# Gated mix of multi-query attention and a state-space convolution on one core: filler matmuls by a shorter history, a burst of dummy matmuls before the scores, two sines as two operations, and gate selectors with a later due time

## The chip, the cores and the metric

The kernel runs on one core of a Trainium2 chip. The metric is the device time of one execution in microseconds; the figure for the kernel before is the median of five executions.

## The reference

From one input x (2048 tokens, 448 channels) two results are computed and mixed by a gate per token.

```
q = (x @ wq) in 16 heads of 28;  k = x @ wk;  v = x @ wv      # one k and one v for all heads
a = softmax(q k^T / sqrt(28)) v, heads joined, @ wo
K[d, l] = Re( sum_n C[d,n] * exp(dt*A[d,n] * l) * dt*B[d,n] )  # 448 channels, 256 complex modes
b = causal convolution of x with K along the tokens + x * Dskip
g = sigmoid(sum(x * gate_w))
out = g * a + (1 - g) * b
```

## The kernel before, in words

Every operation is handed to a planner (class `Prog`) with its engine, an estimated duration, the keys that it reads and writes and a priority `pr` (the lower comes first). `schedule` plays the program through with these estimates and fixes one order for each engine; `emit` writes that order out with the semaphore waits that the keys demand. On the chip each engine then works through its list in order. If an instruction has to wait, everything behind it on that engine waits too.

**Attention.** The scores of 16 heads times 4 query blocks times 16 key tiles make 1024 tiles of 128 by 512. `qk` (L1069) multiplies two or three tiles into one of two PSUM areas (`psS`). One ScalarE instruction takes the exponential of the two or three tiles (L1079), 410 instructions in all. `pv` (L1087) multiplies four of them with v into `psB`, which gathers 16 key tiles of a head group; DVE then copies it out (L1032). `qproj` prepares q for a head group: four matmuls (L729), a reduction of absolute values on DVE into the buffer `Wk` (L734), one more matmul that gives a bound for the softmax (L736), and a copy to `qT` (L738).

**Convolution.** For each of 28 chunks of channels DVE builds tables of powers by doubling (`tables`, L811 to L831), TensorE multiplies them to the kernel K (`kgen`, L846), the result goes through DRAM, and TensorE applies it (`conv`, L914; `jpass`, L889). The planner works the chunks in between the scores. Ahead of this, `seeds_sin` and `seeds` compute sine, cosine and exponentials of dt*A.

**Start.** x is transposed (L541), k is projected (L654), ScalarE copies results out of PSUM (L549, L659). In `seeds_sin` DVE reduces the angle (L595 to L600) and takes its absolute value (L601); ScalarE takes the sine of the angle (L604) and the cosine as a sine of pi/2 less the absolute value (L605). Both sines are one operation for the planner, which starts when L601 is done. A change from Sine to Exp costs a table load on ScalarE.

**Filler.** While `psB` is open (from the first to the last `pv` of a head group), `schedule` puts dummy matmuls (`filler`, L975: four matmuls of zeros by 256 columns) into the planned idle time of TensorE. It does so where the columns worked in the last `FILL_WIN` ns are below `FILL_RATE` columns per ns (1.3 before 75 us of planned time), and where the planned gap is at least the cost of a filler (107 ns, and 112 ns for a change of tile shape) plus `FILL_GAP`.

**Gate.** `prep_gate` computes v and the gate (`mv`, L677), and 28 small matmuls (`mo`, L699 and L704) select and permute the gate values into PSUM bank 5; three DVE operations copy them out (L709, L711, L716), and two DMAs move one of the copies. `conv` uses the same bank later, and its results are scaled by `omq`.

Of the kernel before, what the change touches and what calls it, by code (L numbers as in the profile page):

```python
# [7 lines left out]
AF = mybir.ActivationFunctionType  # L8
# [3 lines left out]
P = 128  # L12
# [6 lines left out]
DT = 112  # L19
# [29 lines left out]
def dram(t, off, dims):  # L49
    return bass.AP(tensor=t.tensor, offset=t.offset + off, ap=[list(d) for d in dims])  # L50
# [7 lines left out]
class Prog:  # L58
# [3 lines left out]
    SWITCH = 112.0  # L62
    LAT = {"pe": 175.0, "act": 105.0, "dve": 105.0}
    LOOK, LOOK_END = {"dve": 200.0}, 26e3
    FILL_NS, FILL_MAC, FILL_WIN, FILL_RATE, FILL_GAP = 107.0, 256.0, 3413.0, 0.47 * 2.4, 130.0
    FILL_WARM = 75e3

    def __init__(self, nc, es):
# [261 lines left out]
def el(n, rate=0.96, fix=69):  # L330
    return fix + n / rate


class Kernel:
# [10 lines left out]
    def build(self):  # L345
        nc = self.nc
        with self.es:
            self.pg = Prog(nc, self.es)
            self.pg.filler = self.filler
            self.alloc()  # L350
            self.consts()
            self.loads()
            self.prep_x()
            self.seeds_sin()
            self.prep_attn()
            self.qproj(0, 0)
            self.seeds()
            self.prep_gate()
            self.main()
            self.pg.schedule()  # L360
            with nc.Block() as block:
                self.pg.emit(block)
# [218 lines left out]
    def seeds_sin(self):  # L581
        pg = self.pg
        self.fT, self.fO, self.fM = self.T.cast(F32), self.O.cast(F32), self.mbf.cast(F32)
        W2 = 2 * D
        t = lambda j: self.tf(j)[0].v(0, P, self.tf(j)[1], [[1, W2]])
        tt = lambda j: self.tf(j)[0].v(0, P, self.tf(j)[1], [[D, 2], [1, D]])
        K = self.tk
        dtb = self.dt32.v(0, P, 0, [[0, 2], [1, D]])
        pg.op("act", lambda e: e.activation(self.fT.v(0, P, 0, [[1, D]]), self.dt32.v(0, P, 0, [[1, D]]), AF.Exp), 600,
              rd=["dt"], wr=[K(0)], pr=-1)  # L590
        pg.op("dve", lambda e: e.tensor_copy(self.dt32.v(0, P, 0, [[1, D]]), self.fT.v(0, P, 0, [[1, 2], [224, 2], [2, DT]])), 540,
              rd=[K(0)], wr=["dt"], pr=-0.5)
        p1, k1, _ = self.trans(1, 6)
        ns = el(W2)
        TT = lambda e, o, a, b, op: e.tensor_tensor(o, a, b, op)  # L595
        pg.op("dve", lambda e: TT(e, tt(1), p1, dtb, ALU.mult), ns, rd=[k1, "dt"], wr=[K(1)], pr=-0.5)
        pg.op("dve", lambda e: e.tensor_scalar(t(2), t(1), 1.0 / TWO_PI, MAGIC, ALU.mult, ALU.add), ns / 2, rd=[K(1)], wr=[K(2)], pr=-0.5)
        pg.op("dve", lambda e: e.tensor_scalar(t(2), t(2), -MAGIC, -TWO_PI, ALU.add, ALU.mult), ns / 2, rd=[K(2)], wr=[K(2)], pr=-0.5)
        pg.op("dve", lambda e: TT(e, t(1), t(1), t(2), ALU.add), ns, rd=[K(1), K(2)], wr=[K(1)], pr=-0.5)
        pg.op("dve", lambda e: e.tensor_scalar(t(1), t(1), -math.pi, math.pi, ALU.max, ALU.min), ns / 2, rd=[K(1)], wr=[K(1)], pr=-0.5)  # L600
        pg.op("dve", lambda e: e.scalar_tensor_tensor(t(2), t(1), -1.0, t(1), ALU.mult, ALU.max), ns, rd=[K(1)], wr=[K(2)], pr=-0.5)  # L601

        def sins(e):
            e.activation(t(3), t(1), AF.Sin)  # L604
            return e.activation(t(4), t(2), AF.Sin, bias=self.small.v(0, P, 3, [[1, 1]]), scale=-1.0)  # L605
        pg.op("act", sins, 4500, rd=[K(1), K(2), "hpi"], wr=[K(3), K(4)], pr=-1)

    def seeds(self):
        pg = self.pg
# [60 lines left out]
    def prep_gate(self):  # L670
        pg = self.pg
        xT = self.xT

        def mv(e):
            for kt in range(16):
                for T in range(NT):
                    r = e.matmul(self.psB.v(0, P, 32 * kt, [[1, 29]]), xT.v(0, DT, T * S + 128 * kt, [[1, 128]]),  # L677
                                 self.Wv.v(0, DT, T * 32, [[1, 29]]), start=(T == 0), stop=(T == 3), tile_position=(0, 0))
            return r
        pg.op("pe", mv, 1900, rd=["Wv"] + [k for c in range(4) for k in self.xk(512 * c)], wr=[("b", 6)], pr=-0.2)  # L680
        pg.op("dve", lambda e: e.tensor_copy(self.vaug.v(0, P, 0, [[32, 16], [1, 28]]),
                                             self.psB.v(0, P, 0, [[32, 16], [1, 28]])), el(448),
              rd=[("b", 6)], wr=["va", ("b", 6)], pr=-0.2)
        gv, ov = self.gtok.v(0, P, 0, [[1, 16]]), self.gtok.v(0, P, 16, [[1, 16]])
        pg.op("act", lambda e: e.activation(ov, self.psB.v(0, P, 28, [[32, 16]]), AF.Tanh, scale=0.5), 150,
              rd=[("b", 6)], wr=["gt"], pr=-0.6)
        pg.op("dve", lambda e: e.tensor_scalar(gv, ov, 0.5, 0.5, ALU.mult, ALU.add), 80, rd=["gt"], wr=["gt"], pr=1.2)
        hi, lo = self.gb.v(0, P, 0, [[1, 16]]), self.gb.v(0, P, 16, [[1, 16]])
        pg.op("dve", lambda e: e.tensor_copy(hi, gv), 80, rd=["gt"], wr=["gb"], pr=1.2)
        pg.op("dve", lambda e: e.tensor_tensor(lo, gv, hi, ALU.subtract), 80, rd=["gt", "gb"], wr=["gb2"], pr=1.2)  # L690
        t, o = self.bank(5)

        def mo(e):
            for k in range(3):
                for rr in range(2):
                    sel = self.J.v(0, P, 64 * rr, [[1, 64]]) if k == 0 else self.ident.v(0, P, 64 * rr - (k - 1), [[1, 64]])
                    for z in range(2):
                        for par in range(2):
                            r = e.matmul(t.v(64 * par, 64, o + 32 * k + 16 * rr, [[1, 16]]), sel,  # L699
                                         self.gb.v(0, P, 16 * z, [[1, 16]]), start=(z == 0), stop=(z == 1),  # L700
                                         tile_position=(0, 64 * par), skip_group_check=True)
            for z in range(2):
                for par in range(2):
                    r = e.matmul(t.v(64 * par, 64, o + 96, [[1, 16]]), self.J.v(0, P, 64 * par, [[1, 64]]),  # L704
                                 self.gb.v(0, P, 16 * z, [[1, 16]]), start=(z == 0), stop=(z == 1),
                                 tile_position=(0, 64 * par), skip_group_check=True)
            return r
        pg.op("pe", mo, 800, rd=["id", "J", "gb", "gb2"], wr=[("b", 5)], pr=1.7, mode="c64")
        pg.op("dve", lambda e: e.tensor_copy(self.gm.v(0, P, 0, [[1, 2], [2, 16]]), t.v(0, P, o, [[16, 2], [1, 16]])), 100,  # L709
              rd=[("b", 5)], wr=["gm"], pr=1.7)  # L710
        pg.op("dve", lambda e: e.tensor_copy(self.gn.v(0, P, 0, [[1, 16]]), t.v(0, P, o + 96, [[1, 16]])), 90,  # L711
              rd=[("b", 5)], wr=["gn"], pr=1.7)
        pg.dma([(dram(self.G, 0, [[1, P], [P, 16]]), self.gn.v(0, P, 0, [[1, 16]]))], (2048, 4), "gw", rd=["gn"], wr=["G"], pr=5, slow=True)
        pg.dma([(self.gn.v(32 * h, 32, 16, [[1, 16]]), dram(self.G, 1536, [[16, 32], [1, 16]])) for h in range(4)],
               (128, 64), "gd", rd=["G"], wr=["gd"], pr=5)
        pg.op("dve", lambda e: e.tensor_scalar(self.omq.v(0, P, 63, [[-32, 2], [-1, 2], [-2, 16]]), t.v(0, P, o + 32, [[32, 2], [16, 2], [1, 16]]),  # L716
                                               -1.0, 1.0, ALU.mult, ALU.add), 130, rd=[("b", 5)], wr=["omq"], pr=1.7)
# [482 lines left out]
```

## Time and profile before

| | |
|---|---|
| median of 5 executions | 524.04 us (521.77 to 524.5) |
| the profiled execution | 524.5 us, of which its span is 522.6 us |
| ACT (ScalarE) busy | 483.4 us, 92% |
| DVE (VectorE) busy | 471.8 us, 90% |
| PE (TensorE) busy | 465.3 us, 89% |
| granted TensorE clock, mean | 0.963 |
| filler matmuls (L975) | 1124 instructions |
| first exponential of the scores | at 27.76 us |

Times are from the start of the span. "Busy" of an engine counts its own instructions, not waits. The granted clock is the share of TensorE's full clock that the throttle let through. "Idle before" is the time for which an engine stood still ahead of an instruction, with what ended it.

### The profile page before, as it was taken

The numbers are of one execution on the slowest core, as the hardware profiler recorded it, in microseconds if no ns is written. First come the engines' busy times: TensorE is split into PE (matmuls) and PEld (weight loads), VectorE is DVE, ScalarE is ACT, GpSimd is POOL, SyncE is SP. The second block draws the span as 40 slices with busy tenths as digits, with TensorE's granted clock in tenths as the row PEclk, the third lists the DMA queues.
The fourth block names the chain that finished last, engine by engine and source line by source line (L and its number), as shares of the span: only waits on it lengthen the run. The fifth ranks groups of instructions, "written<-read, shape, count | busy, mean of one in ns | idle before, by whom it ended". The sixth has DMA issues, their size and how long they took to land.

```text
span 522.6 us, 20724 instructions
## 1 busy us (share of the span) xinstructions
PE 465.3 (89%) x9304; PEld 232.8 (45%) x9304; DVE 471.8 (90%) x1140; ACT 483.4 (92%) x428; POOL 7.5 (1%) x15
## 2 busy tenths in 40 slices
PE   4799888898999989989999899999989899999985
PEld 3442344354534445444444445444444444544434
DVE  4899999999989999999999999999999999997113
ACT  2587999999989999999999999999999999999991
POOL 5000000000000000000000000000000000000000
PEclk9965989999969989999999999999999999999999
DMA  9849700665456436645655765646576746835651
GB/s 196 175 109 125 108 9 11 220 196 175 138 167 179 108 120 193 168 153 140 163 170 150 199 179 165 180 77 186 167 208 171 199 145 178 241 126 189 221 115 37
DMA packets 119279, 80.43 MB, mean 154 GB/s; under 512 B 81825, under 2 KB 87142, under 8 KB 119190
## 3 DMA queue, kind: packets, MB, share of 16 engines
q1 hardware_dynamic: 118166, 78.62, 56.6%
q8 instruction: 73, 1.20, 1.0%
q10 hardware_dynamic: 1024, 0.48, 0.4%
q14 instruction: 16, 0.13, 0.1%
HBM read 73.26 MB, written 5.70 MB: 151 GB/s over the span
## 4 chain that ended last, share of the span: by engine, by line
DVE 53%; ACT 30%; PE 13%; DMA 1%; issue 1%; SPq 0%; DVEq 0%
ACT expT L1079 30%; DVE tab L821 10%; DVE tmp L811 8%; DVE tab L815 8%; DVE tab L829 4%; DVE tab L831 4%; PE psS L1069 3%; DVE cst L923 2%; PE psB L1087 2%; DVE msq L769 2%; PE psX L846 1%; DMA tab<-in_A_x_dram 1%; DVE acc L1032 1%; DVE Wk L734 1%; DVE qT L738 1%; DVE kstg L864 1%
## 5 line engine op out<-in xcount | busy, mean ns | idle before, releaser
L1079 ACT ACTIVATE expT<-psS 128x1536 bf16<-128x1536 f32 (+1 forms) x410 | 468.3, 1258 | 13.1 <-PE psS L1069 6.9
L1069 PE MATMUL psS<-qT,kT 29*128 29x512 bf16 x1024 | 164.4, 397 | 33.7 <-ACT expT L1079 27.9
L1087 PE MATMUL psB<-expT,vaug 128*32 128x512 bf16 x1024 | 104.5, 399 | 0.4 <-ACT expT L1079 0.4
L821 DVE TENSOR_TENSOR tab<-tab,tmp 128x64 bf16<-128x64 bf16 (+1 forms) x280 | 91.1, 365 | 0.8
L1069 PEld LDWEIGHTS psS<-qT,kT 29*128 29x128 bf16 x1024 | 39.4, 91 | 110.9 <-ACT expT L1079 87.4
L914 PE MATMUL psS<-T,U 128*64 128x64 bf16 (+7 forms) x3584 | 85.6, 195 | 0.3 <-issue 0.2
L914 PEld LDWEIGHTS psS<-T,U 128*64 128x64 bf16 (+7 forms) x3584 | 67.4, 107 | 35.1 <-issue 33.9
L811 DVE TENSOR_TENSOR tmp<-tab,mbf 128x128 bf16<-128x128 bf16 (+4 forms) x140 | 80.1, 572 | 0.8
L815 DVE TENSOR_TENSOR tab<-tab,mbf 128x128 bf16<-128x128 bf16 (+4 forms) x140 | 78.9, 569 | 0.0
L846 PE MATMUL psX<-tab 128*32 128x96 bf16 x1792 | 54.9, 267 | 2.4 <-DVE O L894 1.2
L1087 PEld LDWEIGHTS psB<-expT,vaug 128*32 128x32 bf16 x1024 | 26.3, 93 | 61.0 <-issue 59.7
L975 PE MATMUL psB<-kT,zw 128*32 128x256 bf16 x1124 | 50.4, 284 | 0.0
L846 PEld LDWEIGHTS psX<-tab 128*32 128x32 bf16 x1792 | 40.7, 115 | 16.3 <-issue 7.1
L829 DVE TENSOR_TENSOR tab<-tab,mbf 128x2048 bf16<-128x2048 bf16 x28 | 34.3, 1226 | 0.2
L831 DVE TENSOR_TENSOR tab<-tab,mbf 128x2048 bf16<-128x2048 bf16 x28 | 34.2, 1221 | 0.0
L975 PEld LDWEIGHTS psB<-kT,zw 128*32 128x32 bf16 x1124 | 26.9, 98 | 14.6 <-issue 11.3
L923 DVE TENSOR_TENSOR cst<-psS,omq 128x512 bf16<-128x512 f32 x28 | 19.2, 686 | 6.6 <-PE psS L914 6.6
L769 DVE TENSOR_TENSOR msq<-mst 128x448 f32<-128x448 f32 (+2 forms) x45 | 23.9, 531 | 0.0
L729 PE MATMUL psX<-xT,Wq 112*128 112x512 bf16 x64 | 21.3, 409 | 1.1 <-DVE O L618 0.7
L779 DVE CAST mbf<-mst 128x448 bf16<-128x448 f32 (+2 forms) x50 | 17.4, 348 | 0.0
L772 DVE TENSOR_TENSOR mst<-msq 128x224 f32<-128x224 f32 (+2 forms) x50 | 17.2, 345 | 0.0
L775 DVE SCALAR_TENSOR_TENSOR mst<-mst 128x224 f32<-128x224 f32 (+2 forms) x45 | 15.6, 346 | 0.0
(124 smaller groups left out, 270.2 us busy)
## 6 DMA issues: line engine op xcount, KB each, us to landing
T<-KP_scratch SPq DMA_DIRECT2D x224, 256.0 KB, 4.0
rdenB<-R_scratch SPq DMA_DIRECT2D x60, 64.0 KB
tab<-in_A_x_dram SPq DMA_DIRECT2D x8, 224.0 KB, 6.8
XD_scratch<-xT SPq DMA_DIRECT2D x8, 224.0 KB
U<-XD_scratch SPq DMA_DIRECT2D x7, 256.0 KB, 5.4
O<-Z_scratch SPq DMA_DIRECT2D x1, 1792.0 KB, 17.2
KP_scratch<-kstg SPq DMA_DIRECT2D x56, 32.0 KB
U<-XD_scratch SPq DMA_DIRECT2D x7, 192.0 KB, 5.4
```

Of the source, the lines that this page charges most:

```text
L769: pg.op("dve", lambda e, k=k: e.tensor_tensor(msq.v(0, P, 0, [[1, 2 * BW]]) if k > 1 else msq.v(0, P, 0, [[BW, 2], [1, BW]]), src_both(k - ...
L811: pg.op("dve", lambda e, a=src, ra=ra, w=w, so=so: e.tensor_tensor(tmp.v(0, P, so, [[4 * w, 32], [1, 4 * w]]), a, mbf.v(0, P, ra + 4, [[8, ...
L815: pg.op("dve", lambda e, d=dst, a=src, ra=ra, w=w: e.tensor_tensor(d, a, mbf.v(0, P, ra, [[8, 16], [0, 2 * w], [1, 4]]), ALU.mult), el(n, ...
L821: pg.op("dve", lambda e, d=d, t=t2, op=op: e.tensor_tensor(d, d, t, op), el(n // 2, 1.92), rd=[("tmp", lv % 2), ("tab", s, lv + 1)], wr=[( ...
L829: pg.op("dve", lambda e: e.tensor_tensor(ua, src, mbf.v(0, P, ra, [[8, 8], [0, 64], [1, 4]]), ALU.mult), el(2048, 1.92), rd=rk + mk, wr=[( ...
L831: pg.op("dve", lambda e: e.tensor_tensor(ub, src, mbf.v(0, P, ra + BC * 64, [[4, 16], [0, 32], [1, 4]]), ALU.mult), el(2048, 1.92), rd=rk ...
L846: r = e.matmul(self.psX.v(32 * g, 32, 96 * jj, [[1, 96]]), tab.v(0, P, o + 768, [[4, 32]]), tab.v(0, P, o, [[256, 3], [4, 32]]), start=(jj ...
L914: r = e.matmul(ps.v(64 * par, 64 - m, po + 64 * pr, [[1, 64]]), self.U.v(0, P, uo + (32 * par + e0 + pr) * UC + m, [[1, 64 - m]]), self.T. ...
L975: e.matmul(self.psB.v(32 * h, 32, 0, [[1, 256]]), self.zw.v(0, P, 0, [[1, 32]]), self.kT.v(0, P, 0, [[1, 256]]), start=False, stop=False, ...
L1069: r = e.matmul(self.psS.v(0, P, 1536 * s + 512 * k, [[1, 512]]), kT.v(32 * h, DH + 1, 128 * kt, [[1, 128]]), qT.v(32 * h, DH + 1, 512 * qs ...
L1079: pg.op("act", lambda e: e.activation(expT.v(0, P, 512 * (i0 % 10), [[1, n]]), self.psS.v(0, P, 1536 * s, [[1, n]]), AF.Exp, scale=SQ), 61 ...
L1087: r = e.matmul(self.psB.v(32 * h, 32, 0, [[1, 512]]), vaug.v(0, P, 32 * kt, [[1, 32]]), expT.v(0, P, 512 * ((4 * st + h) % 10), [[1, 512]] ...
```

## The change

The constants of the filler rule change. A new function `warm`, called after the first `qproj`, hands the planner five operations of two 512-column matmuls each, whose result in `psB` nobody reads; they read `Wk`, x and the last quarter of k. The two sines become two operations: the first needs the angle alone, the second the absolute value and the first sine. The gate selectors `mo` get a slack of 4000 ns, by which the planner takes their inputs to be ready later than they are.

```diff
-    FILL_NS, FILL_MAC, FILL_WIN, FILL_RATE, FILL_GAP = 107.0, 256.0, 3413.0, 0.47 * 2.4, 130.0
+    FILL_NS, FILL_MAC, FILL_WIN, FILL_RATE, FILL_GAP = 107.0, 256.0, 1700.0, 0.55 * 2.4, 60.0
...
             self.qproj(0, 0)
+            self.warm()
             self.seeds()
...
-        def sins(e):
-            e.activation(t(3), t(1), AF.Sin)
-            return e.activation(t(4), t(2), AF.Sin, bias=self.small.v(0, P, 3, [[1, 1]]), scale=-1.0)
-        pg.op("act", sins, 4500, rd=[K(1), K(2), "hpi"], wr=[K(3), K(4)], pr=-1)
+        pg.op("act", lambda e: e.activation(t(3), t(1), AF.Sin), 2200, rd=[K(1)], wr=[K(3)], pr=-1)
+        pg.op("act", lambda e: e.activation(t(4), t(2), AF.Sin, bias=self.small.v(0, P, 3, [[1, 1]]), scale=-1.0), 2200,
+              rd=[K(2), K(3), "hpi"], wr=[K(4)], pr=-1)
+
+    def warm(self):
+        pg = self.pg
+        for _ in range(5):
+            def warm(e):
+                for h in range(2):
+                    r = e.matmul(self.psB.v(0, P, 0, [[1, 512]]), self.Wk.v(0, DT, 0, [[1, P]]), self.xT.v(0, DT, 0, [[1, 512]]),
+                                 start=True, stop=True, tile_position=(0, 0), skip_group_check=True)
+                return r
+            pg.op("pe", warm, 430, rd=["Wk", ("kT", 3)] + self.xk(0), wr=[("b", 6)], pr=-0.25, mac=1024)
...
-        pg.op("pe", mo, 800, rd=["id", "J", "gb", "gb2"], wr=[("b", 5)], pr=1.7, mode="c64")
+        pg.op("pe", mo, 800, rd=["id", "J", "gb", "gb2"], wr=[("b", 5)], pr=1.7, mode="c64", slack=4000)
```

## The prediction

> **What bounds the kernel now.** I read the page first: three engines at about 90%, and the chain that ended last runs through two of them.
>
> ```profile
> PE 465.3 (89%) x9304; PEld 232.8 (45%) x9304; DVE 471.8 (90%) x1140; ACT 483.4 (92%) x428; POOL 7.5 (1%) x15
> PEclk9965989999969989999999999999999999999999
> DVE 53%; ACT 30%; PE 13%; DMA 1%; issue 1%; SPq 0%; DVEq 0%
> L1079 ACT ACTIVATE expT<-psS 128x1536 bf16<-128x1536 f32 (+1 forms) x410 | 468.3, 1258 | 13.1 <-PE psS L1069 6.9
> ```
>
> ACT works 468.3 us on exponentials and stood idle 13.1 us between them. The granted clock dips four times. So I took windows of one microsecond around each dip. The clock is at 0.5 from about 26 to 29.5, 33 to 50, 67 to 70.5, 145.5 to 156 and 186.5 to 190 us.
>
> ```profile
> 32.00:33.00 1.00, 0.79 (x6) 0.29 (x6) 1.00 (x3) 1.00 (x2) 0.00 (x0) 0.99 0.42 147
> 33.00:34.00 1.00, 1.00 (x8) 0.22 (x7) 1.00 (x3) 0.31 (x2) 0.00 (x0) 0.50 0.39 152
> 49.00:50.00 1.00, 1.00 (x15) 0.26 (x7) 1.00 (x9) 0.35 (x1) 0.00 (x0) 0.50 1.55 164
> 50.00:51.00 1.00, 1.00 (x21) 0.34 (x21) 1.00 (x9) 0.77 (x1) 0.00 (x0) 0.97 0.98 231
> ```
>
> Columns: window, length, busy share of PE, weight loads, DVE, ACT, POOL, then the clock. PE is busy throughout the long spell and ACT is not: there PE is the bound. The timeline of each engine gives the loss. Idle ACT ahead of exponentials: 0.69 + 0.17 + 0.61 + 0.51 + 0.62 + 1.08 + 0.35 + 0.88 = 4.9 us in the spell from 33 us, 0.51 at 71, 0.66 + 0.30 + 0.93 = 1.9 at 150 to 156, 0.23 + 0.20 = 0.4 at 191 to 193. That is 7.7 of the 13.1 us.
>
> But DVE is a second bound. From 157 to 366 us it stands idle for less than 0.1 us in any slice of 13 us, and PE, in order, stands before its tables:
>
> ```profile
> 46.43 0.69 DVE L738 CAST qT<-psX 128x512 bf16<-128x512 f32 x1 [0.76 <-PE psX L736]
> 70.54 0.42 DVE L864 TENSOR_REDUCE kstg<-psX 128x128 bf16<-128x256 f32 x1 [0.52 <-PE psX L853]
> 156.23 0.69 DVE L1032 COPY acc<-psB 128x512 f32<-128x512 f32 x1 [2.38 <-PE psB L1087]
> 477.19 1.22 DVE L831 TENSOR_TENSOR tab<-tab,mbf 128x2048 bf16<-128x2048 bf16 x1
> 478.47 0.35 PE L846 MATMUL psX<-tab 128*32 128x96 bf16 x8 [0.21 <-DVE tab L831]
> ```
>
> The last table ends at 478.41, and its product starts 0.06 us later. I compared the end of L831 with the start of L846 for all 28 chunks: in five of them the product follows within 0.1 us (the first already at 101.8 us), in nineteen within 0.8 us. So an ACT that is some microseconds earlier would mostly wait, by way of PE's order, for tables that are no earlier. What DVE gains reaches the end; what ACT alone gains reaches it only up to those margins.
>
> **Part 1, the sines.** ACT at the start:
>
> ```profile
> 21.15 1.28 ACT L604 ACT_TABLE_LOAD   x1
> 24.57 0.95 ACT L604 ACTIVATE T<-T 128x896 f32<-128x896 f32 x1 [2.13 <-DVE T L601]
> 25.42 1.03 ACT L605 ACTIVATE mbf<-T,small 128x896 f32<-128x896 f32 x1
> 26.47 1.28 ACT L1079 ACT_TABLE_LOAD   x1
> 27.76 1.45 ACT L1079 ACTIVATE expT<-psS 128x1536 bf16<-128x1536 f32 x1
> ```
>
> The angle (L600, from 21.37 for 0.62) is done at 21.99, and the table load at 22.43, so the first sine can run from 22.43 to 23.38. The second still waits for L601, until 24.53. It then takes the first one's place, at 24.57 instead of 25.42: the first exponential comes 0.85 us sooner, at 26.9. Its scores are done at 25.79. No other ACT work lies ready between the two sines (the copy of the last quarter of k ends at 21.14). DVE waits for neither sine today, so DVE gets nothing. By the reading above I count 0 of the 0.85 at the end and keep it for the low end.
>
> **Part 2, the dummy matmuls.** Five times two matmuls of 512 columns. The nearest rows are L654's: four in 1.03 us from 18.30 (0.22 apart) and eight in 3.62 us from 11.59 (0.43 apart), so 2.2 us at full clock or 4.3 at half. They wait on L734, which ends at 23.18. Behind them on PE are:
>
> ```profile
> 23.59 0.39 PE L736 MATMUL psX<-Wk,Wb 128*128 128x512 bf16 x1 [1.83 <-DVE Wb L667]
> 25.19 0.60 PE L1069 MATMUL psS<-qT,kT 29*128 29x512 bf16 x5 [1.21 <-DVE qT L738]
> ```
>
> 0.4 us of the first gap (after 23.18) and the 1.2 of the second hide 1.6 us. The rest, 0.6, falls around the scores, which have a lower `pr` and so give way to one operation at most (0.43); with the first exponential at 26.9 they have 1.1 us to spare. If that cover were gone, the cost is that 0.6 us (2.7 at half clock). It delays `mv` (1.87 us at half clock from 26.29), for which DVE stood 0.78 us at 28.19. At full clock `mv` takes between 0.94 and 1.87 us. Net for DVE between a gain of 0.3 and a loss of 0.6; I take 0. The rewrite of `Wk` comes at 37.57, 11 us later.
>
> The spell from 26 us should go. The one from 33 us need not: the microseconds ahead of it hold transposes, 29-row scores and gaps of 0.43 and 0.74 us, and no filler is allowed before the first `pv` at 32.53.
>
> **Part 3, the fillers.** The needed gap falls from 107 + 112 + 130 = 349 ns to 279. The floor rises from 1.13 to 1.32 columns per ns after 75 us; before that it stays 1.3, but half the history means that a burst (four projections) is sooner forgotten. Price of one:
>
> ```profile
> 47.95 1.68 PE L975 MATMUL psB<-kT,zw 128*32 128x256 bf16 x28
> 57.50 0.95 PE L975 MATMUL psB<-kT,zw 128*32 128x256 bf16 x28
> ```
>
> Seven fillers: 0.24 us each at half clock, 0.135 at full. How many more? At most (1.32 - 1.13) x 13,065 / 256 = 9.8 a slice, some 320 over the 33 slices after 75 us; at least none. PE stood 27.9 us (91 waits) before scores for ACT, room for about 127 at the planner's 219 ns, so I take 150 more, on top of 281: about 1700 records. In those waits they cost nothing; where PE is late they cost 0.135 us each.
>
> What they buy is the clock. DVE idle that half-clock matmuls ended: 0.76 (46.43) + 0.52 (70.54) + 2.38 (156.23) = 3.66 us. Ends: 0, if the same spells come, and 3.66 with the ACT losses on top in the best case. Each spell follows a few microseconds with gaps on PE. Those before 145.5 (0.64 at 143.9, 0.19 at 144.8) lie within a head group and are open to fillers; in the spell from 33 us `psB` is open as well, and more fillers can end it sooner. Those before 67 and 186.5 (0.63 at 65.3, 0.53 at 185.9) lie between two head groups (L1032 at 64.75 and 184.59), where no filler can stand. So I take 2.38 + 0.76 = 3.14 us.
>
> The spell from 33 us follows gaps of 0.43 and 0.74 us at most, and it lasts while PE is busy all the time; so it is the kind of work that counts here, not idle time alone. [...]
>
> **Part 4, the selectors.** 24 + 4 matmuls from 37.69 to 38.61, 0.9 us at half clock. They waited for DVE's read of bank 5 (37.63); 4 us of slack put them at 41.7 or later. They then cost the same elsewhere. The three copies (44.64, 45.35, 47.55) move by up to 4 us, and with them the DMA of `gn`, issued on SP at 48.58; SP's next issue is at 65.47. The first `conv`, which needs the bank, is at 105.6. Covered: 0.
>
> **Sum.** 524.5 (span 522.6 and 1.9 around it) - 3.14 = 521.4 for an execution like the profiled one, which is 0.46 above the median of 524.04. So 520.9.
>
> **Rivals.** About 0.3%, 1.6 us, is what a measurement of this kernel can tell from no change.
>
> *ACT's whole gain arrives.* 7.7 + 0.85 = 8.6 us, median 515.4. It needs the replanned order to leave DVE's tables more room; the margins of 0.06 us speak against it, five chunks with margins over 2.4 us for it.
>
> [...]
>
> *Fillers stand before late scores* (slower). In the regular stretch a group of scores has little to spare: ACT takes 2.24 us a pair (29.11 us for 26 from 480.89), and after ACT frees an area the scores have one 0.92 us exponential to come in. Wherever PE is late (after each wait for a table), extra fillers are pure delay. 3.14 / 0.135 = 23 uncovered fillers cancel the gain; if 55 of the 150 are uncovered, 7.4 us are lost: 520.9 + 7.4 = 528.3. The 27.9 us of waiting speak against it, the smaller gap (70 ns less to spare each time) for it.
>
> **How the numbers follow.** Forecast 0.46, ACT's whole gain 0.14, spells return 0.12, late scores 0.28. Faster 0.46 + 0.14 = 0.60, same 0.12, slower 0.28. The range runs from 514.5 (the best case and 0.9 more) to 528.5 (just past the slower case); I leave out 0.03 below and 0.13 above. The faster cases alone span 514.5 to 522.4.
>
> **What would show it.** Right: the second sine near 24.6 and the first exponential near 26.9; no half clock from 26 to 29.5; the idle DVE before L1032 at 156 gone; about 1700 records of L975; L846 still at L831's heels in most chunks. Wrong: a spell of ten microseconds or more after 33 us; more ACT idle before L1069's scores in the stretches that had a full clock (5.4 us today, 13.1 less 7.7); the last table later than 478.

## The result, and the profile after

The kernel after takes 520.23 us (median of 43 executions, 516.25 to 527.65). Beside it the kernel before took 523.35 (80 executions). The ratio is 0.9934 with a 95% interval of 0.9917 to 0.9952: about 3.5 us faster (the medians differ by 3.1), and the interval leaves out no change.

The execution that was profiled took 523.64 us (span 521.8), which lies in the upper part of the 43. So the two profiles alone hardly differ in time, and that is the first thing to learn here. The page of the kernel after, busy times, clock by 40 slices, chain and exponentials (the line numbers of these lines moved by 9):

```profile
PE 478.3 (92%) x9658; PEld 239.5 (46%) x9658; DVE 471.3 (90%) x1140; ACT 483.3 (93%) x428; POOL 7.5 (1%) x15
PEclk9886689999999969999999999999999999999999
DVE 55%; ACT 26%; PE 14%; DMA 3%; issue 1%; SPq 0%; DVEq 0%
L1088 ACT ACTIVATE expT<-psS 128x1536 bf16<-128x1536 f32 (+1 forms) x410 | 468.2, 1259 | 14.2 <-PE psS L1078 6.6
L984 PE MATMUL psB<-kT,zw 128*32 128x256 bf16 x1468 | 64.4, 281 | 0.0
```

The filler matmuls went from 1124 to 1468, ACT's idle time between exponentials from 13.1 to 14.2 us, and the clock dips as much as before. By its granted clock this execution was at half clock from 22.9 to 29.8, 43.4 to 60.5, 67.3 to 70.7 and 183.4 to 193.6 us: 37.5 us up to the tail (the last microseconds of the span), as in the profile before.

The start, on ACT and then on PE and DVE (timelines: start, length, instruction, idle before):

```profile
21.20 0.95 ACT L603 ACTIVATE T<-T 128x896 f32<-128x896 f32 x1
23.32 1.04 ACT L604 ACTIVATE mbf<-T,small 128x896 f32<-128x896 f32 x1 [1.17 <-DVE T L602]
24.38 1.28 ACT L1088 ACT_TABLE_LOAD   x1
25.72 1.45 ACT L1088 ACTIVATE expT<-psS 128x1536 bf16<-128x1536 f32 x1
```

The first sine no longer waits for the absolute value. Everything in this execution starts about 1.2 us earlier (the last copy of k at 19.20 instead of 20.45), so compare from there: 6.5 us to the first exponential instead of 7.3.

```profile
21.99 0.60 PE L612 MATMUL psB<-xT,Wk 112*128 112x512 bf16 x2 [1.48 <-DVE small L674]
22.43 0.38 PE L745 MATMUL psX<-Wk,Wb 128*128 128x512 bf16 x1
22.65 2.48 PE L612 MATMUL psB<-xT,Wk 112*128 112x512 bf16 x6
25.07 1.03 PE L1078 MATMUL psS<-qT,kT 29*128 29x512 bf16 x5
26.03 1.03 PE L612 MATMUL psB<-xT,Wk 112*128 112x512 bf16 x2
28.80 0.62 DVE L690 CAST vaug<-psB 128x448 bf16<-128x448 f32 x1 [3.84 <-PE psB L686]
```

Six dummy matmuls took 2.48 us, 0.42 apart: half clock. They push the projection of v back, and DVE waits 3.84 us for it where it waited 0.78, as this line of the profile before shows:

```profile
28.19 0.62 DVE L681 CAST vaug<-psB 128x448 bf16<-128x448 f32 x1 [0.78 <-PE psB L677]
```

In this execution the dummy matmuls look like a plain loss.

The windows of one microsecond show the clock falling at 23 us, and again a long spell, here near its ends:

```profile
22.00:23.00 1.00, 1.00 (x5) 0.48 (x6) 0.97 (x2) 0.15 (x1) 0.00 (x0) 0.96 0.40 119
23.00:24.00 1.00, 1.00 (x4) 0.29 (x2) 1.00 (x3) 0.68 (x1) 0.00 (x0) 0.50 0.44 131
44.00:45.00 1.00, 1.00 (x5) 0.10 (x3) 1.00 (x4) 1.00 (x2) 0.00 (x0) 0.50 1.27 99
59.00:60.00 1.00, 1.00 (x10) 0.22 (x10) 1.00 (x3) 1.00 (x1) 0.00 (x0) 0.50 0.97 104
```

At 183 us a spell of 10 us stands where there was one of 3.4, and that at 145 is gone. It costs ACT 0.94 + 0.94 + 0.99 us and DVE 1.01 + 1.10:

```profile
186.46 2.62 ACT L1088 ACTIVATE expT<-psS 128x1536 bf16<-128x1536 f32 x2 [0.94 <-PE psS L1078]
190.02 2.37 ACT L1088 ACTIVATE expT<-psS 128x1536 bf16<-128x1536 f32 x2 [0.94 <-PE psS L1078]
193.38 2.37 ACT L1088 ACTIVATE expT<-psS 128x1536 bf16<-128x1536 f32 x2 [0.99 <-PE psB L1096]
187.52 0.45 DVE L977 SCALAR_TENSOR_TENSOR O<-psX,gm,O 128x224 bf16<-128x224 f32 x1 [1.01 <-PE psX L960]
194.47 0.42 DVE L873 TENSOR_REDUCE kstg<-psX 128x128 bf16<-128x256 f32 x1 [1.10 <-PE psX L862]
```

**Where the time came from is seen over many executions.** Each execution comes with its mean granted clock. Over 90 executions of the kernel before (519.6 to 528.8 us), time and clock go together (the higher the clock, the shorter the time) with a correlation of 0.83: 2.36 us for each 0.01 of clock. 0.01 of a span of 523 us is 5.2 us of lost clock, or 10.5 us at half clock. So one microsecond at half clock goes with 0.23 us of time. (In all means here, executions over 1.5% above the fastest of their kernel are left out, as in the ratios: 9 of 99 of the kernel before, 4 of 56 of the kernel after.) The mean clock was 0.9644 before and 0.9774 after (52 executions): 0.013 x 236 = 3.1 us of the 3.5 that were gained go with the clock. This is a correlation; no run set the clock by itself. The experiments ask which part brings it.

### The profile page after: what moved, and what is told of

Same layout as the page of the kernel before. It is cut to its first block, busy times and chain, and to the rows that moved or that the text cites. A ratio compares the mean times of both kernels' runs of the same rounds, so it can differ in the third digit from the quotient of the medians.

```text
span 521.8 us, 21429 instructions
## 1 busy us (share of the span) xinstructions
PE 478.3 (92%) x9658; PEld 239.5 (46%) x9658; DVE 471.3 (90%) x1140; ACT 483.3 (93%) x428; POOL 7.5 (1%) x15
## 4 chain that ended last, share of the span: by engine, by line
DVE 55%; ACT 26%; PE 14%; DMA 3%; issue 1%; SPq 0%; DVEq 0%
ACT expT L1088 26%; DVE tab L830 10%; DVE tmp L820 8%; DVE tab L824 8%; DVE tab L838 4%; DVE tab L840 4%; PE psS L1078 3%; PE psB L1096 2%; DVE cst L932 2%; DVE msq L778 2%; PE psS L923 2%; DVE O L977 1%; DMA T<-KP_scratch 1%; DVE mbf L788 1%; DMA tab<-in_A_x_dram 1%; DVE Wk L743 1%
## 5 line engine op out<-in xcount | busy, mean ns | idle before, releaser
L1088 ACT ACTIVATE expT<-psS 128x1536 bf16<-128x1536 f32 (+1 forms) x410 | 468.2, 1259 | 14.2 <-PE psS L1078 6.6
L1078 PE MATMUL psS<-qT,kT 29*128 29x512 bf16 x1024 | 164.1, 396 | 19.9 <-ACT expT L1088 12.2
L923 PE MATMUL psS<-T,U 128*64 128x64 bf16 (+7 forms) x3584 | 84.2, 196 | 0.8 <-DMA T<-KP_scratch 0.8
L824 DVE TENSOR_TENSOR tab<-tab,mbf 128x1024 bf16<-128x1024 bf16 (+4 forms) x140 | 79.0, 570 | 0.0
L984 PE MATMUL psB<-kT,zw 128*32 128x256 bf16 x1468 | 64.4, 281 | 0.0
L855 PEld LDWEIGHTS psX<-tab 128*32 128x32 bf16 x1792 | 40.5, 115 | 15.9 <-issue 6.2
L984 PEld LDWEIGHTS psB<-kT,zw 128*32 128x32 bf16 x1468 | 34.9, 97 | 16.4 <-issue 12.4
L1055 DVE TENSOR_TENSOR onT<-acc,rdenB 128x512 bf16<-128x512 f32 x15 | 10.4, 691 | 7.4 <-DMA rdenB<-R_scratch 7.4
```

The costliest lines, as they stand in the source:

```text
L824: pg.op("dve", lambda e, d=dst, a=src, ra=ra, w=w: e.tensor_tensor(d, a, mbf.v(0, P, ra, [[8, 16], [0, 2 * w], [1, 4]]), ALU.mult), el(n, ...
L855: r = e.matmul(self.psX.v(32 * g, 32, 96 * jj, [[1, 96]]), tab.v(0, P, o + 768, [[4, 32]]), tab.v(0, P, o, [[256, 3], [4, 32]]), start=(jj ...
L923: r = e.matmul(ps.v(64 * par, 64 - m, po + 64 * pr, [[1, 64]]), self.U.v(0, P, uo + (32 * par + e0 + pr) * UC + m, [[1, 64 - m]]), self.T. ...
L984: e.matmul(self.psB.v(32 * h, 32, 0, [[1, 256]]), self.zw.v(0, P, 0, [[1, 32]]), self.kT.v(0, P, 0, [[1, 256]]), start=False, stop=False, ...
L1078: r = e.matmul(self.psS.v(0, P, 1536 * s + 512 * k, [[1, 512]]), kT.v(32 * h, DH + 1, 128 * kt, [[1, 128]]), qT.v(32 * h, DH + 1, 512 * qs ...
L1088: pg.op("act", lambda e: e.activation(expT.v(0, P, 512 * (i0 % 10), [[1, n]]), self.psS.v(0, P, 1536 * s, [[1, n]]), AF.Exp, scale=SQ), 61 ...
```

## The experiments

Each part alone, added to the kernel before.

**The filler constants alone.**

```diff
-    ... = 107.0, 256.0, 3413.0, 0.47 * 2.4, 130.0
+    ... = 107.0, 256.0, 1700.0, 0.55 * 2.4, 60.0
```

> The kernel before with the new filler constants alone. Theory A (the fillers shorten the spells at half clock, and the gain is what DVE no longer waits): 2 to 3.5 us faster than before, so ratio 0.993 to 0.996, mean granted clock above 0.963. Theory B (fillers stand before late scores, the gain comes from the other parts): not faster, ratio 1.000 or above, more idle ACT where the clock is full. Theory C (any edit makes the planner write out another order, and that alone moves the time by some microseconds either way): no relation to the clock.

Measured: ratio 1.0003 (0.9962 to 1.0045), mean clock 0.967, 1464 filler matmuls. In its profile there is a spell of 24 us from 30.7 us on. The prediction gave the fillers the whole gain; alone they bring none that shows, though an interval this wide still holds 2 us either way.

**The dummy matmuls alone.**

```diff
             self.qproj(0, 0)
+            self.warm()
...
```

> The kernel before with the ten dummy matmuls alone. Theory A: within 0.6 us of before (ratio 0.999 to 1.001), since they hide in PE's idle time. Rival, from the profile after, where they ran at half clock and DVE waited 3.84 us for the projection of v behind them: 1 to 3 us slower (ratio 1.002 to 1.006).

Measured: ratio 0.9977 (0.9949 to 1.0005), mean clock 0.9745. The rival falls: the kernel is not slower. Theory A's range lies partly within the interval, but the clock is the highest of the four single parts, which that theory did not foresee.

**The two sines alone.**

```diff
-        pg.op("act", sins, 4500, rd=[K(1), K(2), "hpi"], wr=[K(3), K(4)], pr=-1)
+        pg.op("act", lambda e: e.activation(t(3), t(1), AF.Sin), 2200, rd=[K(1)], wr=[K(3)], pr=-1)
+        pg.op("act", ..., 2200, rd=[K(2), K(3), "hpi"], wr=[K(4)], pr=-1)
```

> The kernel before with the two sines as two operations alone. Theory A (DVE's tables set the end): first exponential 0.85 us sooner, time within 0.5 us of before (ratio 0.999 to 1.001). Rival (ACT sets the end): the 0.85 us arrive in full, ratio 0.998.

Measured: ratio 1.0027 (0.9988 to 1.0067), mean clock 0.967. The rival's 0.998 lies just below the interval. ACT's earlier start does not show in the time.

**The slack of the selectors alone.**

```diff
-        pg.op("pe", mo, 800, ..., mode="c64")
+        pg.op("pe", mo, 800, ..., mode="c64", slack=4000)
```

> The kernel before with the slack of the gate selectors alone. Theory A: no change (ratio 0.999 to 1.001). Theory C (a new order alone moves the time): up to 2 us either way.

Measured: ratio 1.0025 (0.9988 to 1.0062), mean clock 0.964. No gain shown.

No single part shows the 0.9934. So the next runs took parts away or together.

**After without the dummy matmuls.**

```diff
             self.qproj(0, 0)
-            self.warm()
```

> The kernel after without the ten dummy matmuls. So far the time of an execution follows its mean granted clock (2.4 us per 0.01 in 35 executions of before), and of the single parts the dummy matmuls had the highest mean clock (0.973 beside 0.963). Theory A (the fillers bring most of the clock): clock near 0.975, time near 521, ratio 0.994 to 0.996. Theory D (the dummy matmuls bring it): clock 0.963 to 0.968, ratio 0.998 to 1.002.

Measured: ratio 0.9949 (0.9918 to 0.998), mean clock 0.9745. Taken alone this speaks for theory A.

**After with the filler constants of before.**

```diff
-    ... = 107.0, 256.0, 1700.0, 0.55 * 2.4, 60.0
+    ... = 107.0, 256.0, 3413.0, 0.47 * 2.4, 130.0
```

> The kernel after with the filler constants of before. Theory A: the gain is gone, clock 0.963 to 0.966, ratio 0.999 to 1.001. Theory D: most of the gain stays, clock 0.971 to 0.975, ratio 0.994 to 0.997.

Measured: ratio 0.986 (0.981 to 0.991) on six executions; the plain means beside it, 518.78 and 524.02 us, differ by 1.0%. The same kernel again:

> The kernel after with the filler constants of before, once more, since its first measurement rests on six executions (ratio 0.986, 0.981 to 0.991). Theory A (the fillers bring the gain): ratio 0.998 or more. Theory D (they are not needed): 0.986 to 0.995, clock 0.973 to 0.977.

Measured: ratio 0.9922 (0.9886 to 0.9957), mean clock 0.980, 1040 filler matmuls. Theory A falls: the kernel without the new filler rule is at least as fast as the kernel after. Whether it is faster is not shown: the first interval lies just below that of the kernel after, the second overlaps it, and the means differ by 1.1 us with a standard error of 0.6.

**Fillers and dummy matmuls, without sines and selectors.**

```diff
-    ... = 107.0, 256.0, 3413.0, 0.47 * 2.4, 130.0
+    ... = 107.0, 256.0, 1700.0, 0.55 * 2.4, 60.0
...
             self.qproj(0, 0)
+            self.warm()
...
```

> The kernel before with the filler constants and the dummy matmuls, without the sines and the slack of the selectors. If the sines and the selectors bring nothing, as both did alone, the clock and the time are those of the kernel after: 0.977, ratio 0.992 to 0.995. If the new order that comes with them matters: ratio 0.997 or more.

Measured: ratio 0.995 (0.9914 to 0.9986), mean clock 0.974, a little under the kernel after. Both expectations are left standing.

**The kernel after once more.**

> The kernel after once more, beside the other three on one chip, for its clock and for a second profile: ratio 0.991 to 0.996, mean clock 0.975 to 0.979. [...]

Measured: ratio 0.9936 (0.9901 to 0.9972), mean clock 0.975. In its profile the clock is halved from 22.6 to 29.4, 43.1 to 60.2, 67.0 to 70.4 and 183.0 to 186.5 us, so at the places of the first profile, and only the last spell has another length. It does not follow that the order of the work sets the places, though: the first spells of the two profiles begin 0.3 us apart (22.9 and 22.6 us), and so do their first dummy matmuls (21.99 and 21.70), so two executions that ran almost alike cannot tell the order from anything else that they share.

The two profiles of the kernel after with the filler constants of before, one kernel with one order of work, say more. One is at half clock from 23.3 to 30.1, 47.2 to 60.8 and 480.7 to 484.1 us, the other from 21.6 to 25.0, 31.8 to 42.1, 62.6 to 69.4, 93.3 to 96.7 and 229.8 to 233.2 us. So the order alone does not set where the spells begin; what else does was not shown. The two ran on different chips.

**Sines and selectors together.**

```diff
+        pg.op("act", lambda e: e.activation(t(3), t(1), AF.Sin), 2200, ...)
+        pg.op("act", ..., 2200, rd=[K(2), K(3), "hpi"], wr=[K(4)], pr=-1)
...
+        pg.op("pe", mo, 800, ..., mode="c64", slack=4000)
```

> The kernel before with the two sines and the slack of the selectors, without fillers and dummy matmuls. If the parts add up, as each alone showed no gain: clock 0.962 to 0.966, ratio 0.999 to 1.005. If the new order that the two give together thins the half-clock spells, which would explain that the kernel after without the dummy matmuls has 0.9745: clock 0.969 or more, ratio 0.995 to 0.998.

Measured: ratio 1.0012 (0.9977 to 1.0047), mean clock 0.962. No gain, and no higher clock.

The kernels with and without one part, all else equal, can now be set side by side (mean time in us, mean clock; equal kernels pooled). The single-part runs and the others lie on three chips, on which the kernel before takes 523.83, 523.83 and 524.02 us, so the chip makes no difference of this size:

| the rest of the kernel | without dummies | with dummies |
|---|---|---|
| as before | 523.89, 0.9644 | 522.17, 0.9745 |
| with the fillers | 523.76, 0.9672 | 521.92, 0.9743 |
| with sines and selectors | 523.66, 0.9621 | 519.22, 0.9795 |
| with all three | 522.25, 0.9745 | 520.34, 0.9774 |

The dummy matmuls gain in all four rows: 1.7, 1.8, 4.4 and 1.9 us, with the higher clock each time. Read down, the same table gives the fillers -0.1 and -0.3 us (first to second row), and -1.4 and +1.1 (third to fourth): nothing steady. Sines and selectors come to -0.2, -3.0, -1.5 and -1.6. A least-squares fit of additive parts to 235 executions says the same: dummies -2.7 us (standard error 0.4) and +0.0089 of clock (0.0013), fillers -0.1 us (0.4). Over all 257 executions, with none left out, the dummies come to -2.7 us (0.5) and the fillers to -0.4 (0.4). With the clock of each of the 235 executions in the fit, the dummies keep 0.6 us (0.2) and the other parts 0.4 or less. So what the dummies gain goes almost wholly with the clock. One kernel does not fit: with all but the dummies the clock is 0.9745, where the additive parts make 0.970; this is left open.

**Earlier dummies**, in the kernel after with the filler constants of before. Do the dummies act by filling the gap ahead of the first scores?

```diff
-    ... = 107.0, 256.0, 1700.0, 0.55 * 2.4, 60.0
+    ... = 107.0, 256.0, 3413.0, 0.47 * 2.4, 130.0
...
-        for _ in range(5):
+        for _ in range(8):
...
-   self.Wk.v(0, DT, 0, [[1, P]]) ... rd=["Wk", ("kT", 3)] + self.xk(0)
+   self.Wq.v(0, DT, 0, [[1, P]]) ... rd=["Wq", ("kT", 3)] + self.xk(0)
```

> The kernel after with the old filler constants, and eight instead of five dummy operations that take their weights from Wq, so that they need not wait for the reduction into Wk and can run from the end of the transposes near 20.5 us on. In the profiles after, the dummy matmuls themselves ran at half clock from 22.6 to 29.5 us, behind a PE idle time of 1.5 us. If that idle time causes the spell: no half clock between 22 and 29 us, 6.8 us less of it (0.0065 of the clock), 1 to 2 us faster than the same kernel with the late ones. If transposes and scores cause it: the spell stays, and the time is the same or up to 1 us more.

Measured: ratio 0.9969 (0.9928 to 1.001), mean clock 0.969. These rest on seven of twelve executions; over all twelve the mean is 524.24 us and the clock 0.959. In its profile (an execution of 526.22 us), PE's timeline and windows of one microsecond:

```profile
23.94 0.60 PE L613 MATMUL psB<-xT,Wq 112*128 112x512 bf16 x2
24.77 1.75 PE L687 MATMUL psB<-Wv,xT 112*128 112x29 bf16 x64
24.00:25.00 1.00, 1.00 (x20) 0.76 (x20) 0.02 (x1) 1.00 (x1) 0.00 (x0) 1.00 0.42 152
28.00:29.00 1.00, 1.00 (x20) 0.76 (x18) 0.65 (x1) 1.00 (x3) 0.00 (x0) 1.00 0.42 147
32.00:33.00 1.00, 1.00 (x9) 0.21 (x7) 1.00 (x3) 0.84 (x1) 0.00 (x0) 0.61 0.43 168
```

The first spell is gone, as expected: full clock until 32 us. The gain is not there: the profile has 44 us of half clock up to the tail, with spells at 291 to 298, 356 to 367 and 394 us among others, and the mean clock is lower than with the late dummies (0.980 with the same other parts). So a full clock at the start is not enough for the gain. Nor does it take early dummies, as the profile of the dummies alone shows:

```profile
21.63 2.12 PE L614 MATMUL psB<-xT,Wk 112*128 112x512 bf16 x8 [1.48 <-DVE small L676]
```

There the late dummies stand behind the same idle time of 1.48 us, run at full clock (0.25 us apart), and the first spell begins only at 35.3 us. So that idle time does not by itself cause the first spell.

The dummies also shift the planned times of all that follows, and the planner then writes out another order. Whether the late dummies' gain is activity at the right moment or an order with fewer thin stretches, these runs do not settle.

**Lighter tables.** Does DVE cap what ACT can gain?

```diff
+        ng = 8 if c < 2 else 4
+        ub = tab.v(0, P, to + 256 + 128, [[1024, ng], [-128, 2], [1, 128]])
+        src2 = tab.v(0, P, qo, [[1024, ng], [1, 256]])
...
```

> The kernel before, in which the last table product of DVE (L831) covers only half its groups from the third chunk on: 26 instructions of 0.6 instead of 1.22 us, so DVE has 16 us less to do, in the same order and with the same planned times. It leaves that half of the tables unwritten. Theory A (DVE's tables cap what ACT can gain): 4 us faster or more (ratio 0.992 or less), since the ACT idle time outside the half-clock spells, 5.5 us, is mostly waits for tables. Theory F (the time goes with what ACT loses in the spells, and DVE hardly matters): within 1.5 us, ratio 0.997 to 1.000.

Measured: ratio 0.9918 (0.9881 to 0.9955), 519.45 us, mean clock 0.966. First the product's group in the profile before, then this run's groups and its chain:

```profile
L831 DVE TENSOR_TENSOR tab<-tab,mbf 128x2048 bf16<-128x2048 bf16 x28 | 34.2, 1221 | 0.0
L834 DVE TENSOR_TENSOR tab<-tab,mbf 128x1024 bf16<-128x1024 bf16 (+1 forms) x28 | 20.1, 716 | 0.0
L1082 ACT ACTIVATE expT<-psS 128x1536 bf16<-128x1536 f32 (+1 forms) x410 | 466.1, 1262 | 9.1 <-PE psS L1072 5.6
ACT 82%; PE 12%; DVE 3%; DMA 1%; issue 1%; SPq 0%; DVEq 0%
```

DVE has 14.1 us less to do (34.2 - 20.1) at nearly the clock of before, and the end comes 4.3 us sooner (0.0082 x 524). ACT's idle time falls from 13.1 to 9.1 us, by about as much; some 3 us of that lie outside the half-clock spells (5.5 us there before, 2.4 now). So late tables do cost time, about 4 us, and DVE is a second bound as the prediction held. But only 4.3 of DVE's 14.1 us reach the end: the chain, 53% DVE before, is now 82% ACT. The clock's price is another thing: 3.2 us per 0.01 (standard error 0.5) in these twelve executions, beside 2.4 (0.2) with the full tables. So nothing shows that half clock is hidden behind the tables.

## Why the prediction was right or wrong

**The number was right, its parts were not.** 520.9 was predicted and 520.23 measured, faster, as forecast. But the sum was 3.14 us for the fillers and 0 for all else, and the table above gives the dummies about 2.5 us and the fillers nothing steady. That the number came out is luck: the gain came from a part that was priced at 0, and two errors offset each other inside the one term for the clock.

- *How much half clock goes.* The sum took away the two spells at 33 and 145 us of the profile, 27 us. The mean clock rose by 0.013, which is 0.013 x 520 / 0.5 = 13.5 us: half of that. Which spells go could not be read from one profile, since one kernel has its spells at different places in two executions.
- *What half clock costs.* The sum priced it by what DVE lost, 3.14 us for 27 us, or 0.12 us for each. The slope of time against clock is 0.23. ACT's own loss in the profile before was 7.7 us in 34 us, 0.23 for each as well. The step that failed, as far as this agreement shows, is "what ACT alone gains reaches the end only up to those margins". The margins were there: in the kernel after, 8 of the 28 products follow their table within 0.1 us. They show that DVE and ACT are both near the bound, not that what ACT gains in a spell is lost in waits later. Nor does all that DVE gains reach the end: of 14.1 us it was 4.3.

**The fillers.** Predicted about 1700 records, found 1468, so 86 fillers more instead of 150. The gaps that they were to fill are not what decides: with 1464 filler matmuls alone the clock was 0.967, with 1040 and the other three parts 0.980. The thin stretch before 43 us and that between head groups at 67 us stayed. The prediction had named the second as out of their reach. The spell from 33 us, which more of them were to end sooner, lasted 17.1 us in the profile before; with the fillers alone one lasted 24 us from 30.7 us on.

**The dummy matmuls.** Priced at 0 because they hide in idle time. Their direct cost was worse than its upper bound of 0.6 us (DVE's wait rose from 0.78 to 3.84 us in the profile), since they ran at half clock. The bound had been taken at full clock; at half it had said 2.7, and 3.06 was found. Where they ran at full clock, in the profile of the dummies alone, DVE waited 1.9 us. Their effect on the rest of the program was not foreseen. The half clock from 26 to 29.5 us, which "should go", stayed in both profiles of the kernel after, and with 6.8 us it lasted twice as long.

**The sines.** The step is confirmed in the profile: 0.8 us from the last copy of k to the first exponential, 0.85 predicted, and no gain of the sines alone at the end.

**The selectors.** They moved from 37.7 to 41.8 us and cost 0.5 us there at full clock; no gain of their own was found.

**The rivals.** Fillers before late scores: not seen. With the fillers alone the ratio is 1.0003, and PE's waits for ACT ahead of scores fell from 27.9 to 12.2 us in the profile after without ACT idling more than 1.1 us longer. That the spells return elsewhere (0.12) was half true: in the profile after one of 10.2 us stands at 183 us, though the mean clock over many executions rose (0.9644 to 0.9774). ACT's whole gain: 516.25 is the fastest execution of the kernel after, and no median came there.

**The signs.** Two of the three signs of being wrong stood in the first profile after, and the number was right all the same: a spell of 17.1 us from 43.4 us, and a last table that ended at 480.9 us, past 478. In the second profile the table ended at 478.4, and the spell was there again. The third did not come: ACT's idle time outside the spells went from 5.5 us (5.4 in the prediction's count) to 5.8.

**Idle gaps.** The fillers bought nothing that shows, yet spells still follow stretches with no long idle gap (0.30 us at most in the 3.4 us before the spell from 43.4 us of the profile after). That the kind of work counts, as the prediction had inferred from the spell at 33 us, no run tested.

## What to carry to other kernels

Before a single profile is priced, look at how its execution lies among the others, and plot time against granted clock: here 3.1 of 3.5 us went with the clock, and two profiles side by side showed none of it. Do not read from one profile which spells will go: the next execution of the same kernel can have others (from 23.3 and 47.2 us here in one, from 21.6 and 31.8 us in another). Price a slow spell by what the engine lost that is fullest over the whole span, not by the one that waits at its end; here that agreed with the measured price. Where a planner writes out the order, an edit that hides in idle time is not free of effect; test each part both added alone and taken away, because no part alone showed what the four did.

## What the runs showed of the hardware

The lengths of the spells in the profiles before and after, at a granted clock of 0.50 and with the tail left out, are 3.4, 6.8, 10.2 and 17.1 us: one, two, three and five times 3.41. In each of the two the spells begin whole numbers of such lengths apart, to within 0.2 us: counted from the first, 2, 12, 35 and 47 in the profile before, 6, 13 and 47 in the profile after. Counted from the start of the span they do not: the first begins at 26.16 us before and at 22.93 us after, 2.3 and 2.5 us past such a multiple, and the spells of the two profiles of the kernel after with the filler constants of before begin about 2.8 and 1.1 us past one. What sets the length and the places was not shown. One order of work gave 516.25 to 523.97 us in the executions compared.

Half clock lasted from 33 to 50 us of the profile before with PE busy for 1.00 of every microsecond, while it worked through 29-row scores, projections and a few fillers. What kind of work keeps the clock was not measured here.

The granted clock reads 1.00 from the start, but its record begins only at 15.9 us in the profile before: from 11.6 us 512-column matmuls came 0.43 us apart, from 18.3 us on 0.22. So the earlier ones came as far apart as the dummy matmuls of the profile after at a granted clock of 0.50 (0.42 us), although the page shows a nine there.
